# Turning q and k of the last chunk by DMA, holding one store behind a transpose, and a new order and layout: a fused transformer layer, forward and backward

## The chip, the cores and the metric

The kernel runs on one core of a Trainium2 chip (trn2). A core has a matrix engine (TensorE, PE in the profile; its weight loads are shown apart as PEld), a vector engine (VectorE, DVE), a scalar engine (ScalarE, ACT), a general engine (GpSimd, POOL) and a sync engine (SyncE, SP), which here only sends out DMA transfers. Each engine works through its own queue of instructions in order; semaphores tie the queues together. Sixteen DMA engines move data for all of them. SBUF is the on-chip memory with 128 partitions, PSUM holds the results of PE in 8 banks, HBM is the memory off the chip.

The metric is the device time of one execution in microseconds (us). Lower is better.

## What is computed

A pre-norm transformer layer over 2048 tokens of width 512, its output, and the gradients of seven of its inputs. Attention has 32 heads of width 16, and each token looks at 8 earlier tokens, two apart. The feed-forward part has 1792 hidden units.

```python
def _A_ref(x, wqkv, wo):                       # H = 32, Dh = 16, W = 8, dil = 2
    qkv = (x @ wqkv).reshape(B, S, 3, H, Dh).transpose(2, 0, 3, 1, 4)
    q, k, v = qkv[0], qkv[1], qkv[2]
    idx = pos[:, None] - (jnp.arange(W) * dil)[None, :]
    mask = idx >= 0
...
    logits = jnp.einsum("bhsd,bhswd->bhsw", q, kg) * scale
    attn = _softmax(jnp.where(mask[None, None, :, :], logits, -1e9), axis=-1)
    o = jnp.einsum("bhsw,bhswd->bhsd", attn, vg)
    return o.transpose(0, 2, 1, 3).reshape(B, S, D) @ wo

def _B_ref(x, w1, b1, w2, b2):
    h = _gelu(jnp.einsum("bsd,df->bsf", x, w1) + b1)
    return jnp.einsum("bsf,fd->bsd", h, w2) + b2

h = x + _A_ref(_layernorm(x), A_wqkv, A_wo)
h2 = h + _B_ref(_layernorm(h), B_w1, B_b1, B_w2, B_b2)
...
_out, _vjp = jax.vjp(_f, A_x, A_wqkv, A_wo, B_w1, B_b1, B_w2, B_b2)
_grads = _vjp(grad_out)                        # all in bf16
```

## The kernel before, in words

**Tiling.** The 2048 tokens are cut into four chunks of 512 (c = 0 to 3; "the fourth chunk" is c = 3, "the second" c = 1). A tile of a chunk is 128 partitions by 4 by 512 numbers of bf16, 512 KB. It is either token-major (a partition is a token) or feature-major (a partition is a feature); between the two lies a transpose, done either by PE in blocks of 128x128 against the identity, with an eviction from PSUM by ACT, or by a DMA that transposes (`dma_start_transpose`, wrapped by `xload`, line 290, always sent out by SP).

**Stages.** For each chunk, `p1_ln` normalises x, `p1_qkv` projects it to q, k and v, `p1_attn` makes the attention weights on VectorE (products) and PE (sums over a head's width), `p1_o` gathers v and makes the attention output, and `p1_h` multiplies by wo and normalises again. `p2_h`, `p2_dg`, `p2_out` and `p2_bwd` are the feed-forward part, forward and backward. `p3_go`, `p3_dots`, `p3_bands` and `p3_gl1` are the attention's backward pass. `wg_ffn` makes the weight gradients. All matrix products of the feed-forward part and of the weight gradients are groups of four or more matmuls on PE. A matmul with 128 columns of weights may be split into four with 32 (`mmul`, line 264), so the profile shows groups of 4 or of 16.

**Tensors in HBM.** The backward pass reads q, k, v and the gradient go as overlapping windows of tokens (`gather`, line 467, sent out by POOL). For that they are stored token-major in HBM: `q_d`, `k_d`, `v_d`, `go_d`. q and k come out of their projection feature-major. `p1_qkv` ends with a loop that turns k and then q: for a pair (name, chunk) in `TMD` (line 1191) by `tm_dma` (line 440), for all others by `to_tm_store` (line 425). Before, `TMD` names only the four chunks of go, so q and k of every chunk go through `to_tm_store`. That is two times per tensor and chunk: eight transposes on PE into one PSUM bank, one eviction of 128x1024 by ACT, one store of 256 KB by SP (`tm_store`).

`tm_dma` has two branches. With an offset of zero it turns the whole tile in one DMA; go takes that. The other branch sends four DMA transposes of 128 KB, one for each 128 features, into one tile, and then one store of 512 KB.

**The attention output.** `p1_o` builds the tile `ost` in four parts (`band`: a product on VectorE, a head sum on PE, a scaled copy by ACT). For the chunks in `FMO` = (1, 3) the finished tile is turned into `oT` by one DMA transpose (`turned`, line 547); PE turns it for the others. Last, `p1_o` stores `ost` to HBM from POOL's queue (line 727), for the weight gradient of wo at the end. `p1_h` multiplies `oT` by wo on PE.

**Order and memory.** Every step above is an operation in a list (`op`), numbered as the code creates it. It carries the engine, and the buffers that it reads (`r`) and writes (`w`), from which its predecessors follow; its costs and `soft` hints serve a planner that is not part of the kernel. The order in which the operations are issued is written out by hand in the tuple `ORDER` (line 1199), one number for each operation; each engine gets its own operations in that order. The place of every buffer in SBUF (in units of 64 bytes) or PSUM (the bank) is written out in `HOMES`. Two buffers that share a place make the later one wait for the last use of the earlier, and since SP works in order, everything behind it in SP's queue waits too.

Of the kernel before, what the change touches and what calls it, by code (L numbers as in the profile page):

```python
# [159 lines left out]
def kernel(  # L160
# [30 lines left out]
    NC = S // CH  # L191
# [39 lines left out]
    ln2_t, o_t = ([dram.tile([P, TPC, D], BF16, name=f"{n}_d{c}") for c in range(NC)] for n in ("ln2", "o"))  # L231
# [12 lines left out]
    sb, ps_, op, fx = pl.sb, pl.ps, pl.op, pl.fixed  # L244
# [40 lines left out]
    def store(dst, ap, src, src_ap, kb, key=None, skey=None, q="SP", tag="store", row=1):  # L285
        e, us = (SY, 0.45) if q == "SP" else (A, 0.45) if q == "ACT" else (G, 0.6)
        return op(q, us, lambda: e.dma_start(out=ap(), in_=src_ap()), r=[(src, skey)], w=[(dst, key)] if dst is not None else (),
                  dma=kb / (DMA_RATE if row <= 1 else WIDE_RATE), tag=tag, piece=0.006 + 0.0385 * row, mode=5)
# [151 lines left out]
    def tm_dma(fm, off, dst, c, back, tag, pm):  # L440

        st = sb("tm" + tag + "d", [P, 4, 512])
        r = c * CH + (RPAD if back else 0)
        if off:
# [268 lines left out]
    def p1_o(c):  # L713
        d = st_[c]
        oT = d["oT"] = sb("oT%d" % c, [P, DC, CH])
# [10 lines left out]
        if c < ORR:  # L726
            store(o_d[c], lambda: o_t[c][:], ost, lambda: ost(), 512, q="POOL", tag="ost", row=4)
# [463 lines left out]
TMD = (('go', 0), ('go', 1), ('go', 2), ('go', 3))  # L1191
# [144 lines left out]
```

## Time and profile before

| what | value |
|---|---|
| median of 3 runs | 551.72 us |
| lowest and highest run | 551.65 and 554.88 us |
| the profiled execution, its own time | 553.64 us |
| its span in the profile | 551.9 us |
| HBM read, written | 55.74 MB, 35.21 MB |
| bytes moved by DMA | 126.68 MB, mean 230 GB/s |

The span is what the profiler sees from the first to the last event; the execution's own time has 1.7 us more around it. "Busy" for PE is modelled, since its matmuls overlap one another, and "clock" is the share of TensorE's full speed that its throttle granted. A line such as `L268 PE MATMUL ps<-wo,oT 128*32 128x512 bf16 x48` reads: line 268 of the kernel, engine PE, what it writes and reads by the program's names, the size of the weights, the size of the moving operand, and how many. A number in brackets behind it is idle time of the engine ahead of it, with what ended it. `SPq` rows are transfers being sent out by SP; the time until the data has landed is given apart, as "to landing".

### The profile page before, as it was taken

Reading aid. Unit: us, or ns where it says so; the run is one execution under the profiler, and the core shown is the slowest. Engines: PE = TensorE matmul, PEld = TensorE weight load, DVE = VectorE, ACT = ScalarE, POOL = GpSimd, SP = SyncE. Lnnn points to the kernel's source line nnn. Section 1 sums busy time; section 2 is a strip of 40 time slices with the busy share of each in tenths; the row PEclk is TensorE's granted clock in tenths of the full one; section 3 lists DMA queues with packets and bytes.
Section 4 is the critical chain, followed back from the end, with each engine's and each line's share of the span. In section 5 each row is a group of like instructions: output and inputs, shape, how many; then the busy total and the mean of one; then the engine's idle time right before and its main releaser. Section 6 shows DMA issues by size and latency. Waiting matters only on the chain.

```text
span 551.9 us, 17462 instructions
## 1 busy us (share of the span) xinstructions
PE 538.8 (98%) x7764; PEld 286.7 (52%) x7764; DVE 494.2 (90%) x648; ACT 324.2 (59%) x507; POOL 25.8 (5%) x40
## 2 busy tenths in 40 slices
PE   7999999999989999999999999999999999999996
PEld 4756554444535445555555555465455555555542
DVE  7999999999979999999787089958899999999993
ACT  4987799989899876885341242034033376443521
POOL 1300100030001000000000000000010001000000
PEclk9999999999989999999999999999999999999999
DMA  8899998991597558679999999999999997888427
GB/s 279 226 291 281 417 302 190 201 332 83 74 235 251 137 98 197 201 121 214 197 191 219 182 194 192 291 218 281 213 279 425 335 338 284 355 290 187 128 60 190
DMA packets 195147, 126.68 MB, mean 230 GB/s; under 512 B 149760, under 2 KB 190656, under 8 KB 193024
## 3 DMA queue, kind: packets, MB, share of 16 engines
q1 hardware_dynamic: 189472, 81.79, 66.3%
q0 software_dynamic: 3408, 41.68, 19.8%
q10 hardware_dynamic: 2192, 2.10, 1.1%
q8 instruction: 60, 0.98, 0.8%
q14 instruction: 15, 0.12, 0.1%
HBM read 55.74 MB, written 35.21 MB: 165 GB/s over the span
## 4 chain that ended last, share of the span: by engine, by line
PE 55%; DVE 16%; ACT 4%; DMA 3%; issue 3%; SPq 2%; POOL 0%; ACTq 0%; DVEq 0%
PE ps L268 32%; PE ps L270 16%; PE ps L527 4%; DMA oT<-ost 2%; DVE xb L856 2%; DVE prbk L518 1%; DVE prbo L518 1%; DVE xb L803 1%; PE ps L487 1%; DVE prbv L518 1%; PE ps L543 1%; DVE x L799 1%; DVE st L360 1%; DVE h L747 1%; DVE h2s L828 1%
## 5 line engine op out<-in xcount | busy, mean ns | idle before, releaser
L479 DVE TENSOR_TENSOR prb<-got,vw 128x4096 bf16<-128x4096 bf16 x16 | 36.0, 2282 | 20.7 <-ACT got L297 13.8
L268 PE MATMUL ps<-w1T,xb 128*32 128x512 bf16 x896 | 53.1, 379 | 0.6 <-DVE h2s L828 0.4
L268 PE MATMUL ps<-goT,w2T 128*32 128x512 bf16 x832 | 50.5, 379 | 0.2 <-ACT xb L774 0.2
L297 ACT CAST wgs<-ps 128x512 bf16<-128x512 f32 (+1 forms) x30 | 16.2, 562 | 53.8 <-PE ps L270 30.4
L268 PE MATMUL ps<-w,gl 128*32 128x512 bf16 x776 | 46.3, 379 | 0.0
L856 DVE SCALAR_TENSOR_TENSOR xb<-xb,ps 128x512 bf16<-128x512 bf16 x56 | 36.9, 681 | 6.6 <-PE ps L268 6.4
L774 ACT ACTIVATE xb<-ps,b1c 128x512 bf16<-128x512 f32 x56 | 35.6, 703 | 10.1 <-PE ps L268 5.0
L268 PEld LDWEIGHTS <-xb 128*32 128x32 bf16 x896 | 26.2, 97 | 23.1 <-issue 1.2
L518 DVE TENSOR_TENSOR prbv<-Rv,cfv 128x4096 bf16<-128x4096 bf16 x16 | 35.7, 2284 | 1.4 <-PE ps L527 1.4
L518 DVE TENSOR_TENSOR prbq<-Rq,cfq 128x4096 bf16<-128x4096 bf16 x16 | 35.9, 2287 | 0.9 <-PE ps L270 0.4
L518 DVE TENSOR_TENSOR prbk<-Rk,cfk 128x4096 bf16<-128x4096 bf16 x16 | 35.9, 2284 | 0.3 <-PE ps L527 0.2
L518 DVE TENSOR_TENSOR prbo<-Ro,cfo 128x4096 bf16<-128x4096 bf16 x16 | 35.9, 2283 | 0.2
L479 DVE TENSOR_TENSOR prf<-qt,kt 128x4096 bf16<-128x4096 bf16 x16 | 35.7, 2283 | 0.0
L268 PEld LDWEIGHTS <-w2T 128*32 128x32 bf16 x832 | 24.0, 97 | 21.3 <-issue 0.5
L268 PEld LDWEIGHTS <-gl 128*32 128x32 bf16 x776 | 21.3, 97 | 21.1 <-ACT gl L777 1.3
L268 PE MATMUL ps<-wqkvT,gqkvT 128*32 128x512 bf16 x512 | 31.0, 379 | 0.0
L796 ACT ACTIVATE xb<-xb 128x2048 bf16<-128x2048 bf16 (+1 forms) x16 | 26.6, 1691 | 6.4 <-DVE xb L795 6.4
L626 PE MATMUL ps<-ln1T,wqk 128*32 128x512 bf16 x512 | 29.3, 381 | 0.7 <-ACT ln1T L297 0.7
L270 PE MATMUL ps<-ln2T,w 128*128 128x512 bf16 x120 | 27.4, 379 | 0.0
L792 ACT ACTIVATE x<-xb 128x2048 bf16<-128x2048 bf16 (+1 forms) x16 | 26.4, 1691 | 1.4 <-DVE h L747 1.3
L777 ACT ACTIVATE gl<-xb 128x2048 bf16<-128x2048 bf16 (+1 forms) x16 | 26.5, 1686 | 0.1
L561 ACT ACTIVATE gyr<-ps,rstd 128x512 bf16<-128x512 f32 x16 | 10.8, 677 | 23.5 <-PE ps L268 23.5
(199 smaller groups left out, 1085.7 us busy)
## 6 DMA issues: line engine op xcount, KB each, us to landing
Ro<-v_d POOLq DMA_DIRECT2D x4, 2304.0 KB, 11.6
Rq<-k_d POOLq DMA_DIRECT2D x4, 2304.0 KB, 11.5
Rv<-go_d POOLq DMA_DIRECT2D x4, 2304.0 KB, 13.9
Rk<-q_d POOLq DMA_DIRECT2D x4, 2304.0 KB, 14.1
g_d<-gl SPq DMA_DIRECT2D x9, 512.0 KB, 5.2
gh_d<-xb SPq DMA_DIRECT2D x9, 512.0 KB, 4.7
w<-in_B_w_dram SPq DMA_DIRECT2D x2, 1792.0 KB, 7.4
out_dram<-wgs SPq DMA_DIRECT2D x13, 256.0 KB, 4.7
```

The costliest lines, as they stand in the source:

```text
L268: T.matmul(out[32 * a:32 * a + 32, :], lhsT=l[:, 32 * a:32 * a + 32], rhs=r, start=start, stop=stop, skip_group_check=True)
L270: T.matmul(out, lhsT=l, rhs=r, start=start, stop=stop, skip_group_check=True)
L297: fn = lambda: A.copy(out=ap(), in_=pap())
L479: op("DVE", tt_us(4096), lambda g=g, pr=pr: V.tensor_tensor(out=pr(), in0=ql()[:, g, :].unsqueeze(1).to_broadcast([P, W, 512]), in1=_sub(k ...
L518: V.tensor_tensor(out=pr().rearrange("p a j (d h) -> p a j d h", h=H), in0=_sub(R()[:, o0, 0:1], [[st, 2], [512, 4], [32, DH], [1, H]]), i ...
L527: T.matmul(ps()[32 * j:32 * j + 32, :], lhsT=S4[:], rhs=pr()[:, hf, j, :], start=(hf == 0), stop=(hf == 1), skip_group_check=True)
L626: T.matmul(ps()[32 * a:32 * a + 32, gg * 512:(gg + 1) * 512], lhsT=_sub(wq_()[:, dc, 0:1], [[DH, H]], sel * D + 4 * g + a), rhs=rhs, start ...
L774: op("ACT", act_us(512, 1), lambda f=f, ps=ps, xb=xb, f0=f0: A.activation(out=xb()[:, f - f0, :], in_=ps(), func=ACT.Identity, bias=b1c[:, ...
L777: op("ACT", act_us(N), lambda xb=xb, gl=gl: A.activation(out=fl(gl), in_=fl(xb), func=ACT.Gelu_apprx_tanh), r=[xb], w=[gl], tag="gelu", mo ...
L792: op("ACT", act_us(N), lambda xb=xb, x2=x2: A.activation(out=fl(x2), in_=fl(xb), func=ACT.Square), r=[xb], w=[x2], tag="x2")
L796: op("ACT", act_us(N), lambda xb=xb: A.activation(out=fl(xb), in_=fl(xb), func=ACT.Tanh, scale=GC), w=[xb], tag="tanh", mode=6)
L856: op("DVE", 0.61, lambda f=f, ps=ps, z=z, f0=f0: V.scalar_tensor_tensor(out=z()[:, f - f0, :], in0=z()[:, f - f0, :], scalar=1.0, in1=ps() ...
```

## The change

Three things change in the code, and the two tuples are replaced.

- `TMD` gains ('q', 3) and ('k', 3). For these two, `tm_dma` takes its branch with four DMA transposes. The condition of that branch is now whether the tensor is q or k, since q has an offset of zero too. Twelve operations become ten: four groups of eight transposes on PE, four evictions on ACT and four stores of 256 KB on SP go; eight DMA transposes of 128 KB and two stores of 512 KB on SP come.
- `store` takes a list of further reads. The store of `ost` of the fourth chunk now also reads `oT`, so it waits on POOL until the DMA transpose of `ost` has landed.
- `ORDER` (1970 operations instead of 1972) and `HOMES` (883 buffers instead of 889) are new throughout. Operations made after the fourth chunk's q have numbers lower by two.

```diff
@@ -282,9 +282,9 @@
-    def store(dst, ap, src, src_ap, kb, key=None, skey=None, q="SP", tag="store", row=1):
+    def store(dst, ap, src, src_ap, kb, key=None, skey=None, q="SP", tag="store", row=1, more=()):
         e, us = (SY, 0.45) if q == "SP" else (A, 0.45) if q == "ACT" else (G, 0.6)
-        return op(q, us, lambda: e.dma_start(out=ap(), in_=src_ap()), r=[(src, skey)], w=[(dst, key)] if dst is not None else (),
+        return op(q, us, lambda: e.dma_start(out=ap(), in_=src_ap()), r=[(src, skey)] + list(more), w=[(dst, key)] if dst is not None else (),
                   dma=kb / (DMA_RATE if row <= 1 else WIDE_RATE), tag=tag, piece=0.006 + 0.0385 * row, mode=5)
@@ -441,7 +441,7 @@
         st = sb("tm" + tag + "d", [P, 4, 512])
         r = c * CH + (RPAD if back else 0)
-        if off:
+        if tag in "qk":
             for g in range(4):
                 xload(st, lambda g=g: st()[:, :, g * P:(g + 1) * P], lambda g=g: fm()[:, g, off:off + CH], 128, r=[(fm, g // 2)], key=g, tag="tmx" + tag)
             store(dst, lambda: dst()[r:r + CH, :].rearrange("(a p) d -> p a d", p=P), st, lambda: st(), 512, key=(c, 0), tag="tmst" + tag)
@@ -724,7 +724,7 @@
         d["ost"] = ost
         if c < ORR:
-            store(o_d[c], lambda: o_t[c][:], ost, lambda: ost(), 512, q="POOL", tag="ost", row=4)
+            store(o_d[c], lambda: o_t[c][:], ost, lambda: ost(), 512, q="POOL", tag="ost", row=4, more=[oT] if c == NC - 1 and c in FMO else ())
@@ -1188,7 +1188,7 @@
-TMD = (('go', 0), ('go', 1), ('go', 2), ('go', 3))
+TMD = (('go', 0), ('go', 1), ('go', 2), ('go', 3), ('q', 3), ('k', 3))
...
```

Read by their numbers, the operations that SP has round the transposes of `ost` stand as follows in the two orders (first sent first):

| round | before | after |
|---|---|---|
| second chunk's `oT` | w2 transpose, v store, x load, **oT**, three q stores, k store, q store | q transpose, w2 transpose, **oT**, x load, k store, two q transposes, q store |
| fourth chunk's `oT` | three stores of h2, w1 transpose, **oT**, w1 transpose, a small store, w1 transpose | x load, two stores of h2, x load, gelu store, x load, **oT**, w1 transpose, a small store, w1 transpose |

On PE, the operations between the last head sum of the fourth chunk's `ost` and its first matmul on `oT` are ten groups of four matmuls in the old order and thirteen in the new one. Between the same two points of the second chunk, the new order has one such group less. Ahead of the first matmul on the first chunk's `ghT` (the turned gradient in the backward pass), counted from the VectorE operation that completes its source, there were 24 groups' worth and there are now 8.

205 rows, old and new, of tables (HOMES, ORDER) are left out of this document.

## The prediction

> **What bounds the kernel now.** I read the page first, then the busy time by stretch, then the chain in order of time, and last the timelines of TensorE (PE), SP and GpSimd (POOL) round the one place where PE stands still.
>
> ```profile
> span 551.9 us, 17462 instructions
> PE 538.8 (98%) x7764; PEld 286.7 (52%) x7764; DVE 494.2 (90%) x648; ACT 324.2 (59%) x507; POOL 25.8 (5%) x40
> PE 55%; DVE 16%; ACT 4%; DMA 3%; issue 3%; SPq 2%; POOL 0%; ACTq 0%; DVEq 0%
> ```
>
> PE is busy for 98% of the span and carries most of the chain. So nearly every microsecond that leaves PE's work or its waits leaves the time, and nearly every new wait enters it. The stages differ, though. Busy us of each engine by stretch, then granted clock, DMA share and GB/s:
>
> ```profile
> core 0: us, PE busy (x) PEld busy (x) DVE busy (x) ACT busy (x) POOL busy (x), PEclk, DMA share, GB/s
> 80.00:100.00 20.00, 19.97 (x233) 9.55 (x231) 19.91 (x15) 19.76 (x27) 0.60 (x1) 1.00 0.87 180
> 100.00:120.00 20.00, 19.75 (x198) 9.81 (x199) 19.37 (x29) 19.62 (x25) 3.03 (x3) 1.00 0.99 268
> 154.00:156.00 2.00, 0.06 (x4) 0.06 (x8) 2.00 (x3) 1.99 (x2) 0.00 (x0) 1.00 1.35 145
> 156.00:158.00 2.00, 2.00 (x24) 0.85 (x28) 0.92 (x6) 2.00 (x2) 0.00 (x0) 0.58 0.80 174
> ```
>
> Between 80 and 120 us PE, DVE and ACT are all full. At 154 us PE does nothing for 2 us, and afterwards its clock is granted at 0.58. The chain says what it waited for:
>
> ```profile
> 126.40 1.24 DVE xb L803
> ...
> 129.70 3.61 PE ps L270 x16
> ...
> 145.99 9.90 DMA oT<-ost
> 155.94 44.55 PE ps L268 x788
> ```
>
> Up to 128 us the long pieces of the chain are DVE's, then PE's, then comes one transfer of 9.90 us, and after it PE again. That transfer is the DMA transpose of the fourth chunk's attention output (`turned`). Its surroundings on PE, SP and POOL:
>
> ```profile
> 144.70 0.62 PE L527 MATMUL ps<-prbo,S 128*32 128x512 bf16 x8
> 145.13 1.91 PE L268 MATMUL ps<-ln2T,w 128*32 128x512 bf16 x32
> ...
> 148.59 2.78 PE L268 MATMUL ps<-ln2T,w 128*32 128x512 bf16 x48
> 151.18 2.80 PE L268 MATMUL ps<-goT,w2T 128*32 128x512 bf16 x48
> 155.94 4.46 PE L268 MATMUL ps<-wo,oT 128*32 128x512 bf16 x48 [1.96 <-DMA oT<-ost]
> 160.22 1.04 PE L268 MATMUL ps<-goT,w2T 128*32 128x512 bf16 x16
> ```
>
> ```profile
> 143.87 1.51 SPq L291 DMA_TRANSPOSE w1T<-in_B_w_dram  x1
> 145.99 3.40 SPq L291 DMA_TRANSPOSE oT<-ost  x1
> 149.43 5.95 SPq L291 DMA_TRANSPOSE w1T<-in_B_w_dram  x1
> ```
>
> ```profile
> 146.26 0.59 POOL L287 DMA_DIRECT2D o_d<-ost  x1 [22.34 <-ACT ost L532]
> ```
>
> The transpose is sent out 2.1 us behind a transpose of w1 and 0.27 us ahead of the 512 KB store of the same tile.
>
> **The change, part by part.** *The wait at 154 us.* It costs twice. PE waits 1.96 us. Then 48 matmuls take 160.22 - 155.94 = 4.28 us, where 48 took 151.18 - 148.59 = 2.59 us: 1.69 us more at the lower clock. Together 3.65 us. The change acts on it in three ways. The store now waits for the transpose. In SP's new order (read by operation numbers) no w1 transpose is sent ahead of this one; a load of x and a store of gelu's output stand there, both free to leave long before, and the w1 transposes come behind. And PE's new order has 13 groups of four matmuls (each cut into 16 narrow ones) between the last head sum of the chunk and the first matmul on oT, not 10. A group takes 0.865 us (160 narrow ones from 145.13 to where 151.18 and its 48 would end, 153.77), so the cover grows from 8.65 to 11.2 us. The transpose leaves 0.86 us after PE is through with the head sum (145.13 to 145.99). Even with 9.90 us it lands after 10.8 us, inside 11.2. So I take the whole 3.65 us; the other end is 0, if it lands 2.6 us later than before.
>
> The skill gives another size. The Trainium skill, "TensorE: Matmul & The Clock Gate", section "HAM oscillation — how this bites in real kernels", warns of PE gaps above about 3.4 us. By that the clock would survive a gap of 1.96 us, the wait would be worth 2.0 us and the sum would end 1.7 us higher. The trace differs: clock 0.58 after the 1.96 us gap; the measurement decides.
>
> *The store's wait on POOL.* It leaves some 4 us later at the first chunk's landing time below. Behind it on POOL is only the power of the fourth chunk's second layernorm, which needs the very matmuls that read oT and so cannot run before the transpose has landed. The stored tile is read back in the last stage. I cost it at nothing; its cover is that distance, and without it the store's 0.59 us of issue would be the price.
>
> *Transposes off PE.* Sixteen 128x128 transposes each for q and k go, in four operations of 8.
>
> ```profile
> 88.45 0.61 PE L434 MATMUL ps<-ident,qt 128*128 128x128 bf16 x8
> 88.89 3.40 PE L270 MATMUL ps<-ln2T,w 128*128 128x512 bf16 x15
> ```
>
> ```profile
> L297 ACT COPY tmq<-ps 128x1024 bf16<-128x1024 bf16 x8 | 8.2, 1036 | 2.0 <-PE ps L434 2.0
> ```
>
> Each occupies PE for 88.89 - 88.45 = 0.44 us: 1.8 us in all. They lie in the first 130 us, where the chain is mostly DVE's. Counting the two orders, DVE has the same instructions ahead of the chunk's last product, plus two tiny ones. PE has the four operations less and one group more ahead of the last head sum. If that head sum comes at the same time, what is left of PE's work is one group shorter: 0.87 us. If PE sets that time, it is 1.8. I take 0.9, by the DVE rows of the chain; the ends are 0 and 1.8.
>
> *Evictions off ACT.* Four of 1.036 us (the row of q's; k's are the same copy): 4.1 us less, in a stage where ACT is 98% busy. Who waits there:
>
> ```profile
> DVE nm L376 <- POOL rstd L373: 0.3, 1, 0.3
> ACT xb L774 <- PE ps L270: 2.3, 4, 1.3
> ```
>
> From 80 to 145 us DVE waits for nobody worth naming, and ACT's longest wait is for PE. Full as it is, ACT is not what DVE waits for. I take 0; the other end is a gain of 4.1.
>
> *Eight DMA transposes on SP.* They move 1 MB from SBUF to SBUF; four stores of 256 KB become two of 512 KB. The trace has no transpose of 128 KB out of SBUF. The nearest are got's, of 512 KB:
>
> ```profile
> L291 SPq DMA_TRANSPOSE tmgod<-got x4: 1987/3050/9741, 320.4 to 380.9; - x4
> DMA to landing us min/median/max: 4.6/6.1/13.3
> ```
>
> ```profile
> L287 SPq DMA_DIRECT2D q_d<-tmq x8: 478/577/1548, 47.9 to 112.2; - x8
> ```
>
> One costs SP between 0.5 us (a quarter of the shortest) and 3.05 us (the median), eight of them 4 to 24 us, less two stores, 1.2 us. The results are wanted only by gathers of the last attention backward stage. What matters is who stands behind them in SP's queue: for k the load of w2, for q the transposes of w2 and of grad_out and, tightest, the second chunk's oT. Before, that was
>
> ```profile
> 107.57 1.90 SPq L291 DMA_TRANSPOSE oT<-ost  x1
> DMA to landing us min/median/max: 4.3/4.3/4.3
> 113.76 1.03 PE L270 MATMUL ps<-wo,oT 128*128 128x512 bf16 x4
> 114.62 0.62 PE L416 MATMUL ps<-ident,ln 128*128 128x128 bf16 x8
> ```
>
> It lands at 111.87, 1.9 us before PE comes to it. The new order has one group (114.62 - 113.76 = 0.86) less between, so the margin is 1.0 us. At 4.3 us it holds; I take 0. If it took 13.3 us like the slowest of got's, PE would wait 13.3 - (112.90 - 107.57) = 8.0 and lose 1.7 at the lower clock: the end is +9.7.
>
> *New order and homes.* Elsewhere the stages keep their sequence. Covers that shrank: eight groups (6.9 us) before the first matmul on ghT, where there were 24. Its landing times:
>
> ```profile
> DMA to landing us min/median/max: 4.5/5.3/6.2
> ```
>
> Still inside, by 0.7 us at worst; taken as 0, with 3.7 us at the other end, if it comes as late as oT did and the clock falls with it.
>
> *The sum.* The profiled execution took 553.64 us, 1.7 around its span: 553.64 - 1.96 - 1.69 - 0.9 = 549.1. The median of the runs, 551.72, lies 1.9 below that execution; whether it waits less or the profile adds time is not to be seen, so I take off half, 1.0: 548.1, rounded to 548.0, which is 0.7% under the median.
>
> **The rivals.** *ACT was what held the first stage.* For it: 19.76 and 19.62 us busy of 20. Against it: DVE's 19.91 and 19.37, and the waits. It would give the whole 4.1 us more: 543.9.
>
> *A tighter cover gives way a little.* The second chunk's oT lands in 9.9 us, as the fourth's did, with two q transposes and one of w2 ahead of it: wait 9.9 - 5.3 = 4.6 and 1.7 of clock, 548.0 + 6.3 = 554.3. Or ghT comes as late as the fourth chunk's oT did: 551.7.
>
> *The wait stays.* The w1 transpose behind oT, not the store or the one ahead, made it slow, and it gets slower by the cover that was added. Then only 0.9 goes: 551.7. Against it: the 9.90 us began with one w1 transpose ahead and the store beside, and both are gone.
>
> *Slower: SP's queue in the first stage.* The q transposes hold up SP and the DMA engines so that the second chunk's oT takes 13.3 us: 548.0 + 9.7 = 557.7. It decides from 557.2 on, a landing of 12.8 us. For it: the DMA share 0.99 there, the 9.74 us that one of got's held SP. Against: the q transposes are a quarter as large, and that one left 1.3 us behind a gather:
>
> ```profile
> 379.60 0.53 POOL L471 DMA_DIRECT2D Rv<-go_d  x1 [26.81 <-DVE prbq L518]
> 380.88 9.74 SPq L291 DMA_TRANSPOSE tmgod<-got  x1
> ```
>
> The Trainium skill speaks for it: "VectorE: DVE Perf Modes", section "The three transpose paths", has 390 ns for a 128x128 block on TensorE and 1309 ns by DMA, and its rules prefer TensorE where PSUM will do; no row here prices one such block.
>
> **How the numbers follow.** About 1% is what a measurement of this kernel can tell from no change. Forecast, 546.2 to 551: 0.45. ACT held the stage, below 546.2: 0.22. A cover gives way a little, 551 to 555: 0.15. The wait stays, about 551.7: 0.06. Slower, above 557.2: 0.12. Faster by over 1% (under 546.2) is the second with 0.04 from the forecast's lower edge, where the median runs had the full wait and PE the full 1.8: 0.26. Slower 0.12; within 1% the remaining 0.62. The range 543.9 to 554.3 leaves out the slower case and little else; the likeliest case's own is 546.2 to 551.
>
> **What would show it.** Right: no idle time of PE before the first matmul on the fourth chunk's oT, granted clock 1.00 from 140 to 180 us, the store on POOL some 4 to 10 us behind the transpose's issue; PE's count lower by 32; oT's last head sum within 1 us of 145. Wrong: PE idle before the second chunk's oT near 113 us, or before ghT near 310, with a clock under 1 behind it; SP busy without a break from 60 to 115 us; or a last head sum well before 144, which would say that ACT was the limit.

## The result: slower, and the profile after

| | median | runs |
|---|---|---|
| before | 552.56 us | 4 runs, 551.65 to 554.88 |
| after | 559.77 us | 4 runs, 557.50 to 563.47 |
| after over before | 1.0142 | 95% interval 1.0112 to 1.0173 |

The forecast was 548.0 us, 543.9 to 554.3. The profiled execution of the changed kernel took 559.96 us.

Ratios here are taken over runs within 1.5% of a kernel's fastest; the ranges below give every run, since the changed kernel and most of its variants scatter upwards by 10 us and more, while the 72 runs of the kernel before beside them, on the same chips, lie between 551.0 and 558.0 us.

The page of the changed kernel (span; busy time, share of the span and number of instructions):

```profile
span 558.2 us, 17856 instructions
PE 538.5 (96%) x7948; PEld 291.0 (52%) x7948; DVE 492.7 (88%) x648; ACT 320.4 (57%) x503; POOL 24.4 (4%) x40
```

PE has as much work as before (538.5 against 538.8 us). The 6.3 us of the span are idle time and clock. Windows of 40 us tell where. Before, then after (busy time of PE in the second column, then PEld, DVE, ACT, POOL; granted clock, DMA share, GB/s):

```profile
0.00:40.00 40.00, 35.57 (x409) 22.15 (x410) 35.97 (x64) 31.69 (x45) 6.96 (x12) 1.00 0.88 270
120.00:160.00 40.00, 37.92 (x426) 18.46 (x428) 37.06 (x54) 35.70 (x51) 2.00 (x2) 0.96 0.59 127
280.00:320.00 40.00, 39.76 (x740) 22.04 (x736) 20.95 (x54) 12.11 (x34) 0.00 (x0) 1.00 1.18 202
320.00:360.00 40.00, 40.00 (x465) 20.31 (x458) 36.79 (x36) 7.68 (x15) 0.60 (x1) 1.00 1.08 233
```

```profile
0.00:40.00 40.00, 37.68 (x448) 23.16 (x452) 36.64 (x67) 30.28 (x44) 4.98 (x12) 1.00 0.91 271
120.00:160.00 40.00, 37.34 (x433) 18.60 (x432) 36.73 (x54) 35.78 (x50) 2.00 (x2) 1.00 0.86 209
280.00:320.00 40.00, 38.43 (x715) 21.15 (x708) 23.94 (x54) 16.02 (x35) 0.00 (x0) 1.00 1.17 199
320.00:360.00 40.00, 33.40 (x498) 17.26 (x494) 28.12 (x27) 7.63 (x14) 0.60 (x1) 0.96 1.15 225
```

From 320 to 360 us PE idles 6.60 us where it idled for none, and the clock of 0.96 takes 40 x 0.04 = 1.6 us more: 8.2 us, more than the whole loss. They have two causes: 4.85 us of the idle time are one wait for VectorE's glf, and 1.75 us, ahead of it, one for gw2in. From 120 to 160 us the clock is back at 1.00 (1.6 us gained), but PE idles 2.66 us, 0.6 more than before, although the 1.96 us ahead of oT are gone. 280 to 320 us lose 1.3, the first 40 us gain 2.1. The other windows and the tail come to about nothing between them. PE's waits in the changed kernel name the culprits (total, times, longest):

```profile
PE ps L268 <- DVE glf L927: 4.9, 1, 4.9
PE ps L527 <- DVE prbo L518: 2.6, 2, 2.2
PE ps L270 <- DMA gw2in<-g_d: 1.7, 1, 1.7
...
PE ps L270 <- DMA oT<-ost: 0.4, 1, 0.4
```

**The forecast's own place.** The fourth chunk's oT: SP, POOL, PE.

```profile
147.13 2.91 SPq L291 DMA_TRANSPOSE oT<-ost  x1
```

```profile
147.40 0.59 POOL L287 DMA_DIRECT2D o_d<-ost  x1 [23.58 <-ACT ost L532]
```

```profile
158.01 1.91 PE L268 MATMUL ps<-wo,oT 128*32 128x512 bf16 x32
```

PE comes to oT 10.9 us after the transpose was issued and waits for nothing. The store, though, leaves 0.27 us behind the start of the transpose, as before, and was released by ACT: the added read sets the store's place in the written order and gives it no wait on the transpose.

**The new wait near 346 us.** SP, then DVE, of the changed kernel:

```profile
334.73 1.03 SPq L287 DMA_DIRECT2D go_d<-tmgod  x1
335.81 5.53 SPq L291 DMA_TRANSPOSE gw2in<-g_d  x1
341.44 8.48 SPq L291 DMA_TRANSPOSE gw1in<-gh_d  x1
350.02 1.70 SPq L287 DMA_DIRECT2D go_d<-tmgod  x2
```

```profile
341.54 4.48 DVE L479 TENSOR_TENSOR prb<-got,vw 128x4096 bf16<-128x4096 bf16 x2
353.74 1.22 DVE L927 TENSOR_TENSOR glf<-ps,attn 128x1024 bf16<-128x1024 f32 x1 [7.71 <-DMA go_d<-tmgod]
```

glf has nothing to do with tmgod. It lies on it: in the new HOMES the first two chunks' tmgod tiles (units 225 to 289 and 352 to 416) overlap glf (272 to 416). Before, they lay at 2614 and 32. So VectorE waits until the second tile's store is through, and that store stands behind two transposes that hold SP for 14 us. PE waits for glf:

```profile
355.02 3.33 PE L268 MATMUL ps<-gor,gw2in 128*32 128x512 bf16 x32 [4.85 <-DVE glf L927]
```

The 32 matmuls behind the wait take 3.33 us at the lower clock, where the 32 at 158.01 above take 1.91. An estimate from these lines: the wait for glf costs 4.85 + 1.42 = 6.3 us of the 8.2.

**The new wait near 130 us.**

```profile
111.61 3.96 SPq L291 DMA_TRANSPOSE tmqd<-qt  x2
...
116.69 0.59 SPq L282 DMA_DIRECT2D gor<-in_grad_out_dram  x1
128.73 0.37 SPq L287 DMA_DIRECT2D q_d<-tmqd  x1
129.15 1.18 SPq L287 DMA_DIRECT2D k_d<-tmk  x1
```

```profile
132.75 2.15 DVE L497 STREAM_TRANSPOSE cfo<-attn 128x512 bf16<-128x512 bf16 x2 [2.15 <-DMA k_d<-tmk]
```

The same pattern. cfo's new place overlaps the first chunk's old k tile (tmk). The store that frees it is behind q's store on SP, and that one waited 11.4 us for the turned q: SP sent nothing from 117.3 to 128.73.

### The profile page after: what moved, and what is told of

It is laid out like the page before. It is cut to its first block, busy times and chain, and to the rows that moved or that the text cites. A ratio compares the mean times of both kernels' runs of the same rounds, so it can differ in the third digit from the quotient of the medians.

```text
span 558.2 us, 17856 instructions
## 1 busy us (share of the span) xinstructions
PE 538.5 (96%) x7948; PEld 291.0 (52%) x7948; DVE 492.7 (88%) x648; ACT 320.4 (57%) x503; POOL 24.4 (4%) x40
## 4 chain that ended last, share of the span: by engine, by line
PE 50%; SPq 3%; DVE 2%; ACT 1%; DMA 1%; issue 0%; DVEq 0%
PE ps L268 31%; PE ps L270 13%; PE ps L527 4%; SPq L291 3%; PE ps L543 1%; PE ps L487 1%; ACT woT L1130 1%; DVE xb L856 1%; DMA go_d<-tmgod 1%; DVE u L566 0%; DVE glf L927 0%; DVE x L799 0%; SPq L287 0%; ACT gyr L561 0%; PE ps L919 0%
## 5 line engine op out<-in xcount | busy, mean ns | idle before, releaser
L479 DVE TENSOR_TENSOR prb<-got,vw 128x4096 bf16<-128x4096 bf16 x16 | 36.0, 2284 | 10.9 <-ACT got L297 10.3
L268 PE MATMUL ps<-gor,gw2in 128*32 128x512 bf16 x560 | 34.4, 391 | 4.9 <-DVE glf L927 4.9
L268 PEld LDWEIGHTS <-w2T 128*32 128x32 bf16 x832 | 24.7, 97 | 23.4 <-issue 4.2
L561 ACT ACTIVATE gyr<-ps,rstd 128x512 bf16<-128x512 f32 x16 | 10.9, 682 | 43.8 <-PE ps L268 39.1
L268 PEld LDWEIGHTS <-gl 128*32 128x32 bf16 x792 | 23.8, 97 | 19.4 <-issue 0.5
L268 PE MATMUL ps<-ln2T,w 128*32 128x512 bf16 x464 | 28.1, 379 | 0.0
L268 PEld LDWEIGHTS <-gw2in 128*32 128x32 bf16 x560 | 16.9, 99 | 19.6 <-issue 6.6
```

Of the source, the lines that this page charges most:

```text
L268: T.matmul(out[32 * a:32 * a + 32, :], lhsT=l[:, 32 * a:32 * a + 32], rhs=r, start=start, stop=stop, skip_group_check=True)
L479: op("DVE", tt_us(4096), lambda g=g, pr=pr: V.tensor_tensor(out=pr(), in0=ql()[:, g, :].unsqueeze(1).to_broadcast([P, W, 512]), in1=_sub(k ...
```

## The experiments

All runs, each beside the kernel before on the same chip (its medians there: 552.2 to 552.8 us):

| kernel | median, us | runs | lowest and highest, us |
|---|---|---|---|
| a_unchanged, a_unchanged2 (the changed kernel) | 570.7, 569.6 | 6, 6 | 557.9 to 584.5, 557.3 to 577.5 |
| a_store_ahead | 567.5 | 6 | 556.0 to 594.5 |
| a_q_store_behind | 573.7 | 6 | 560.8 to 577.6 |
| a_both | 569.1 | 11 | 553.0 to 588.8 |
| a_glf_free | 574.2 | 6 | 565.5 to 595.4 |
| a_q_early | 572.9 | 6 | 562.6 to 598.3 |
| a_fixed | 573.3 | 6 | 563.6 to 578.8 |
| a_plain | 559.4 | 6 | 557.5 to 563.9 |
| a_plain_glf | 553.2 | 13 | 550.4 to 576.3 |
| a_q_plain, a_k_plain | 564.3, 567.8 | 6, 6 | 556.1 to 571.7, 562.5 to 573.9 |
| a_pe_turns | 563.1 | 4 | 562.4 to 565.0 |
| a_pe_turns_glf | 555.8 | 5 | 554.5 to 556.2 |
| b_turns, b_turns2 | 561.5, 568.4 | 6, 6 | 555.9 to 574.5, 556.4 to 571.3 |
| b_plain | 557.7 | 6 | 555.4 to 567.1 |
| b_w1_behind | 553.1 | 12 | 552.3 to 556.4 |

The first variants scattered by up to 38 us, so the changed kernel was run again beside the next ones. It runs from 557.3 to 584.5 us; its first four runs were the lower end. A theory must explain the scatter too.

### Stores moved in SP's queue

```diff
 ORDER   # a_store_ahead: the second chunk's go_d store (1246) ahead of a gw1in transpose (1767)
-..., 1767, ..., 1246, ...
+..., 1246, 1767, ...
 ORDER   # a_q_store_behind: the q_d<-tmqd store (440) seven rows back, behind an h2 store (577)
-..., 440, ..., 577, ...
+..., 577, 440, ...
```

> The changed kernel with one DMA moved in SP's queue: the second chunk's go_d<-tmgod store goes ahead of the gw1in transpose that held SP for 8.48 us, nothing else. Theory 'laid over': VectorE's glf multiply waits 7.71 us only because glf lies on the place of that store's tile; the store is issued at about 341.5 instead of 350.0 us, lands before 347, VectorE's wait is under 1 us, PE's 4.85 us and the clock under 1 behind it go. PE was idle 6.6 us in 320 to 360 and lost about 1.6 more at clock 0.96, so the time falls by 4.9 to 8.2 us, to 551.5 to 555 where the changed kernel takes 559.8. Rival 'full queue': SP has too many transposes in that stretch; PE then waits as long for gw2in or gw1in, pushed back by the store, and the time stays at 557 or more.

> The changed kernel with the q_d<-tmqd store (512 KB, the fourth chunk's q) moved seven rows back in SP's queue, behind the k_d store, the h2 stores and the loads it stood in front of. Theory 'laid over': VectorE's 2.15 us before cfo and 0.57 us before a prbo go, PE's 2.2 us before bsum with them; the last head sum comes 1.5 to 2.7 us sooner and the time is 557 to 558.5 where the changed kernel takes 559.8. Rival 'the turn itself is late': the transposes of q land 12 to 16 us after issue, and the store, now seven rows back, releases tmqd's own place later: VectorE waits for q_d<-tmqd instead and the time is 559.5 or more.

> Both moves of the two runs above in one kernel. Theory 'laid over': the gains add, 559.8 - (4.9 to 8.2) - (1.3 to 2.7) = 549 to 553.6, middle 550.6: between no difference and 0.7% under the kernel before. The rivals: as one of them alone, or 557 and more.

By their medians all three fell on the rival's side. Under this scatter that is a weak test. In a_both a small gain isn't excluded: by its ratio it is at 1.0077 of the kernel before (1.0044 to 1.0109), the changed kernel at 1.0142 (1.0112 to 1.0173) in its first four runs and at 1.0128 (1.0056 to 1.0200) in a_unchanged2, on other chips. In a_store_ahead's profile, where VectorE waits 7.5 us before cfo and all behind it is about 9 us later:

```profile
350.73 0.62 SPq L287 DMA_DIRECT2D go_d<-tmgod  x1
351.45 11.14 SPq L291 DMA_TRANSPOSE gw1in<-gh_d  x1
```

```profile
362.73 1.23 DVE L927 TENSOR_TENSOR glf<-ps,attn 128x1024 bf16<-128x1024 f32 x1 [7.32 <-DMA go_d<-tmgod]
```

The store leaves ahead of the transpose now, and VectorE waits as long: it goes on 12.0 us after the issue, where it went on 3.7 us after it with the store behind (350.02 to 353.74 above). The DMA engines are full there (share 1.10 from 351 to 362 us), and the store is through when the transpose has been issued. So an earlier row of the queue needn't be an earlier landing. How much later is not general: stores of this kind issued behind the transposes took 9.2 us to land in a_pe_turns's profile, 9.6 in a_unchanged's and 10.0 in a_unchanged2's. In a_q_store_behind's profile, which is of its fastest run (560.8), the wait before cfo is gone and a wait of 1.5 us before prbo stands in its place; five of its six runs were above 572 us.

### glf's place freed

```diff
 HOMES   # a_glf_free, of the two tmgod tiles and of two prb tiles
-tmgod 225, tmgod 352, prb 1329, prb 1345
+tmgod 224, tmgod 1329, prb 288, prb 288
```

> The changed kernel with four homes changed and nothing else: the second chunk's tmgod tile goes from 352 to 1329, two prb tiles to 288 for it, the first chunk's tmgod tile from 225 to 224, so that glf (272 to 416) lies on the first chunk's tile alone, whose store is issued 15 us earlier. A side effect: the gather Rq (1185 to 1473) now waits for the second chunk's store, and starts near 350 instead of 340.79 us. Theory 'laid over': VectorE's wait before glf (7.71, 7.32, 6.93 us in the three profiles) falls under 1 us, PE loses under 2 us between 340 and 360 instead of 6.6, the clock stays at 1.00 there; 4.9 to 8.2 us less than the changed kernel in like runs, 551.5 to 555 against 559.8. Rival 'the transfers are the limit': PE waits as long for gw2in, or the gather comes late for prbq near 373; less than 2 us is gained.

> The changed kernel itself once more, beside the variants on the same chip, for its spread. Both theories: a median of 557 to 564 as in its first four runs (557.5 to 563.5). Theory 'the q turn is late': some runs lie far above, up to 590, since the landing of the q transposes (15.7 us in its first profile, 21.8 in a run of 567.6) sets when VectorE goes on near 130 us. Theory 'laid over alone': all runs within 4 us of each other, since the order and the places are the same in each.

The two from 320 to 400 us, a_unchanged first:

```profile
320.00:360.00 40.00, 38.10 (x669) 18.93 (x662) 24.61 (x22) 14.98 (x30) 0.60 (x1) 1.00 1.17 195
360.00:400.00 40.00, 34.80 (x368) 19.39 (x369) 30.91 (x30) 8.40 (x19) 0.32 (x1) 0.96 0.99 224
```

```profile
320.00:360.00 40.00, 39.84 (x677) 21.89 (x670) 26.68 (x23) 14.98 (x30) 0.00 (x0) 1.00 1.18 204
360.00:400.00 40.00, 39.12 (x502) 21.57 (x505) 35.37 (x33) 10.52 (x25) 1.13 (x2) 1.00 1.14 268
```

PE works 6.1 us more in these 80 us, and the clock keeps its 1.6. VectorE's wait for the store before glf, 5.92 us in a_unchanged, is gone: the place was its cause. Whether the total fell, six runs of each can't show, since those of either kernel lie 27 to 30 us apart; the cleaner pairs follow below. Another wait is far longer in these runs. VectorE, a_unchanged, and the landing times of q's turns (tmqd) and of the gathers of v (Ro) in the same profile:

```profile
145.68 2.15 DVE L497 STREAM_TRANSPOSE cfo<-attn 128x512 bf16<-128x512 bf16 x2 [12.24 <-DMA k_d<-tmk]
```

```profile
L291 SPq DMA_TRANSPOSE tmqd<-qt x4: 1202/1659/2655, 99.0 to 116.5; - x4
DMA to landing us min/median/max: 2.5/13.6/26.4
```

```profile
DMA to landing us min/median/max: 10.6/13.0/26.1
```

The 2.15 us at cfo are 12.24 here (9.9 in a_glf_free's profile). A q transpose and a gather of 2304 KB in flight beside it both take 26 us. In the first profile of the changed kernel the slowest of each took 15.7 and 15.4. Where the places and the order around q are the same, the time of the profiled run rises with the slowest of q's transposes: 15.7 us at 560.0, 18.8 at 563.1 (a_unchanged2), 21.8 at 567.6 (a_store_ahead), 22.8 at 571.0 (a_k_plain), 26.4 at 575.1 (a_unchanged). And a_unchanged2, on another chip, runs as long as a_unchanged, so it isn't one chip.

### q's turns sent earlier

```diff
 ORDER   # a_q_early; a_fixed is this with the homes of a_glf_free
-..., 439, ..., 437, ..., 436, ...
+..., 439, 437, 436, ...
```

> The changed kernel with two rows of SP's queue moved: the last two transposes of q go up beside the first two, ahead of the w2 transpose and the second chunk's oT, some 10 us before the 2304 KB gather is issued. Theory 'the q turn is late': all four have landed by 118, the q_d store is issued before 120 instead of 128.7, VectorE's wait before cfo (2.15 us, 7.5 us in a run of 567.6) goes and the long runs with it: the runs lie within 4 us of each other at 556 to 559. Its price: the second chunk's oT starts 2.4 us later, PE waits 0.4 to 2.8 us for it. Rival: the transfers are as slow wherever they are put; the landing stays at 13 us or more and the runs stay spread over 10 us and more.

> The places of a_glf_free and the order of a_q_early in one kernel. If both theories hold, the gains add: 559.8 - (4.9 to 8.2) - (1 to 2.7) = 549 to 554, with runs within 4 us of each other, at or under the kernel before (552.4). Rival 'the transfers are the limit': 555 and more.

q's turns land within 2.6 us there (3.7 in a_fixed), so their place counts. But nothing is won: 572.9 and 573.3. Ahead of oT they make PE wait 2.8 us for it, and other stores come late (VectorE's h waits 5.9 us for a k_d store, PE 4.8 us for w). The crowding moved to k's turns: the gather issued beside them at 73.9 us landed after 17.1 us in a_q_early's profile (570.8) and 23.4 in a_fixed's (578.8), where it took 9.5 in the first profile of the changed kernel. Why it meets them there is open.

### Copies in place of the turns

```diff
@@ tm_dma   # a_plain; a_q_plain and a_k_plain for one tensor only
-xload(st, lambda g=g: st()[:, :, g * P:(g + 1) * P], lambda g=g: fm()[:, g, off:off + CH], 128, ...)
+op("SP", 0.4, lambda g=g: SY.dma_start(out=st()[:, :, g * P:(g + 1) * P],
+     in_=fm()[:, g, off:off + CH].rearrange("p (a d) -> p a d", d=P)), ...)
```

> The changed kernel, with the eight transposes of q and k replaced by eight plain copies of the same 128 KB, in the same rows of SP's queue, with the same tiles, waits and stores. The copies don't turn the data, so the fourth chunk's q and k reach DRAM unturned: that part is left out. Theory 'turns load the transfers': a DMA transpose of 128 KB keeps the DMA engines busy far longer than a copy, in a stage where they are busy all the time already; without it the waits between 80 and 160 us go, and with them the spread: runs within 4 us of each other at 552 to 556, the wait before glf (6 to 8 us) still there. Rival 'rows and places': SP's extra rows, the places held longer and the new order make the waits, however the bytes are moved: median above 560, spread over 10 us as in the changed kernel (557.9 to 584.5 beside its variants).

> The same copies, and the four homes of a_glf_free. Theory 'turns load the transfers' together with 'laid over': the wait before glf goes too, 5 to 8 us less than a_plain: 546 to 550, under the kernel before (552.7). Rival 'rows and places': above 556. Rival 'the transfers are the limit' in the backward stage: within 2 us of a_plain.

The direction is the theory's, the size is not: 559.4 where 552 to 556 was expected. a_plain from 120 to 160 us, and its copies of q, then of k:

```profile
120.00:160.00 40.00, 39.13 (x470) 19.75 (x472) 38.70 (x59) 37.78 (x55) 2.00 (x2) 1.00 0.74 211
```

```profile
L446 SPq DMA_DIRECT2D tmqd<-qt x4: 644/664/680, 96.2 to 111.1; - x4
DMA to landing us min/median/max: 2.6/3.8/4.5
```

```profile
L446 SPq DMA_DIRECT2D tmkd<-kt x4: 612/659/696, 60.5 to 73.1; - x4
DMA to landing us min/median/max: 3.3/7.6/11.8
```

For k the landing is nearly that of the transposes in the first profile of the changed kernel:

```profile
DMA to landing us min/median/max: 4.0/8.4/12.9
```

So copies land sooner at q's place only; at both, SP issues one in 0.7 us where a transpose took 1.2 or more.

PE's idle time falls from 2.66 to 0.87 us (in a_unchanged PE was busy for 27.50 of the 40), and the scatter from 27 us to 6.4, over the 4 us expected. The median is 11 us below a_unchanged and 10 below a_unchanged2 (both on other chips), and level with the changed kernel's first four runs. With glf's place free as well, 6.3 us go: 553.2, ratio to the kernel before 1.0015 (0.9992 to 1.0037). Three of its 13 runs lay above 572, and the profile caught one (572.6 us). SP and PE there:

```profile
380.21 29.33 SPq L291 DMA_TRANSPOSE gw1in<-gh_d  x1
```

```profile
413.18 3.61 PE L268 MATMUL ps<-gw1in,ln 128*32 128x512 bf16 x32 [16.63 <-DMA gw1in<-gh_d]
```

One transpose, which the kernel before has too, held SP for 29.33 us, while a gather issued at 377.3 us was in flight; the slowest gather of that kind (Rv) landed after 32.2 us. So the scatter isn't q's alone. Every profile above 563 us shows a transpose that is stretched beside a stretched gather: q's beside the gather of v (a_unchanged, a_unchanged2, a_store_ahead, a_glf_free, a_k_plain), k's (a_q_early, a_fixed), here gw1in's, in b_turns2 below two of the backward stage. That the pairing makes the long runs is argued from these profiles, not shown: the kernel before sends its transpose of the turned gout (tmgod) beside the same gather Rv, where it held SP for 9.74 us and landed after 13.3, and its runs do not scatter so.

> The changed kernel with the four transposes of q replaced by plain copies (q of the fourth chunk reaches DRAM unturned); k's four transposes stay. Theory 'turns load the transfers', with q's beside the gather of 100 to 125 us as the worst of it: 559 to 562, spread under 6 us, as with all eight replaced (557.4 to 563.9). Rival 'k's turns do it': they fill the DMA queues from 60 to 75 us and the stores behind them come late: median above 563, spread over 10 us.

> The changed kernel with the four transposes of k replaced by plain copies (k of the fourth chunk reaches DRAM unturned); q's four transposes stay. Theory 'q's beside the gather': median above 563 and a spread over 10 us, nearly as in the changed kernel. Rival 'k's turns do it': 559 to 562, spread under 6 us.

> The changed kernel itself beside these three on one chip, as their base. Theory 'turns load the transfers': median 558 to 572 with runs over 10 us apart; the rival 'one chip was slow': within 3 us of 559.8, as in its first four runs.

All on one chip: copies for q leave 564.3, copies for k 567.8, all turned 569.6, each with runs 11 to 20 us apart. Neither theory wins. Of each pair of forecasts the one with the high median came true: q's turns alone bring the scatter back, and so do k's; the 3.5 us between the two medians are far inside the scatter. a_k_plain's profile (571.0) loses its time at q's place, with VectorE's wait of 9.0 us before cfo. Which stage made the high runs of a_q_plain was not seen; its profile is of a run of 556.1 with a clean first stage.

### The new order with TensorE's turns

```diff
 TMD   # a_pe_turns; a_pe_turns_glf has the homes of a_glf_free too
-(..., ('go', 3), ('q', 3), ('k', 3))
+(..., ('go', 3))
 HOMES
-tmkd 1921, tmqd 1070
+tmk 1921, tmk 1953, tmq 1070, tmq 1102 (PSUM banks 0, 6, 5, 6)
```

> The new order and homes, but the fourth chunk's q and k turned by TensorE as before (four groups of PE transposes, four evictions on ACT, four stores of 256 KB), in the places and near the rows of the transposes: the second part of the change without the first. Theories 'turns load the transfers' and 'laid over': no waits in the first stage, oT's wait of 3.65 us with its clock gone as predicted, the wait before glf there: 552.7 - 3.65 + (5 to 8) = 554 to 557, spread under 4 us. Rival 'rows and places': the first stage waits as in the changed kernel: above 560.

> The same with the four homes of a_glf_free: new order, turns by TensorE, glf's place free. Both theories: 554 to 557 less 5 to 8 = 547.5 to 551, that is 0.3% to 1% under the kernel before, spread under 4 us: the version that should beat both kernels. Rival 'the transfers are the limit' in the backward stage: within 2 us of a_pe_turns.

The code of the kernel before, with the new order and homes. No DMA transposes of q and k, no scatter: 2.5 and 1.7 us from lowest to highest. And freeing glf's place gives 563.1 - 555.8 = 7.3 us, the cleanest measure of it; PE is busy for 40.00 us from 320 to 360. But both lie above what was expected, a_pe_turns_glf at 1.0060 of the kernel before (1.0047 to 1.0073). It loses 2.5 us from 80 to 120 us, PE's waits for the evictions of the turned q and k (1.8 and 1.2 us), whose places in the order were my choice, and 2.4 from 280 to 320. The version that was to beat both does not.

### The kernel before, one part changed

```diff
 TMD   # b_turns; b_plain the same with copies
+('q', 3), ('k', 3)
 HOMES
-tmk 993, tmk 1025, tmq 416, tmq 448
+tmkd 993, tmqd 416
 ORDER   # b_w1_behind: one w1 transpose (511) behind the fourth chunk's oT (476) and the next w1 transpose
-..., 511, ..., 476, ..., 510, ...
+..., 476, ..., 510, 511, ...
```

> The kernel before with the turn of q and k alone: eight DMA transposes and two stores for the fourth chunk's four PE turns, four evictions and four stores, in the places of the old tiles, the eight transposes spread over SP's rows from 326 to 380 of the old order; the order and homes of all else as before. By the prediction's step the turn is worth 0.9 (0 to 1.8) us: 550.8 to 552.6 where the kernel before takes 552.6. Rival 'ACT held the first stage': 4.1 us off ACT come back as well, 547.5 to 549. Rival 'SP held up': w2T, the second chunk's oT or other rows come late behind the transposes, PE waits before them, 554 to 562.

> The kernel of b_turns (the kernel before with q and k of the fourth chunk turned by DMA, its own order and places), with the eight transposes replaced by plain copies of the same 128 KB in the same rows: q and k reach DRAM unturned. Theory 'turns load the transfers': without the turning the first stage stands as before: 551 to 554, spread under 4 us, at most 1% from the kernel before (552.4). Rival 'rows and places': eight more rows on SP, and kt's and qt's places held until a transfer has read them, cost the same however the bytes are moved: 558 to 563 like b_turns.

> b_turns once more beside it on the same chip, as its base. Theory 'turns load the transfers' and rival alike: a median of 558 to 565 and a spread over 10 us, as it had (555.9 to 574.5).

Turned by DMA, in the old order, the kernel takes 561.5 and 568.4 us. With copies on the chip of the latter it takes 557.7, 10.8 us less in the median, and 5.0 us remain without any turning. The ratios overlap (1.0138, 1.0080 to 1.0196, against 1.0086, 1.0063 to 1.0108): what the turning itself adds is mostly the high runs. How it adds them is open. b_turns2's profile (568.5) does not lose its time at the turns of q and k: up to 400 us PE idles 14.0 us, in b_plain 13.7. From 400 to 440 us PE is busy for 31.60 us at a clock of 0.91. SP and VectorE there:

```profile
385.39 20.77 SPq L291 DMA_TRANSPOSE tmgod<-got  x1
```

```profile
409.69 1.15 DVE L497 STREAM_TRANSPOSE cfq<-glf 128x512 bf16<-128x512 bf16 x1 [13.94 <-DMA tmgod<-got]
```

That is a transpose which the kernel before has too, beside the gather Rv issued at 383.33, which landed after 23.0 us. The 5.0 us that remain with copies are in VectorE, b_plain:

```profile
99.83 2.29 DVE L518 TENSOR_TENSOR prbo<-Ro,cfo 128x4096 bf16<-128x4096 bf16 x1 [4.00 <-DMA tmkd<-kt]
```

prbo waits until a transfer has read kt, whose place it takes. (In b_turns the same wait is 5.2 us.) So the rival "rows and places" holds for the 5 us. b_turns too came out in the range of its rival "SP held up" (554 to 562), though by this place and not by the second chunk's oT, for which PE waits 1.7 us.

> The kernel before with one row of SP's queue moved: the w1 transpose that stood ahead of the fourth chunk's oT goes behind it; no change of places, turns, store or cover. Theory 'the transpose ahead': that transpose (issued 2.1 us ahead, on the same DMA engines) made oT land after 9.9 us; without it oT lands in 5 to 8 us, inside the cover of 8.65, PE's wait of 1.96 us and the clock of 0.58 and 0.57 behind it go: 552.4 - 3.65 = 548.8, 548 to 550. Rival 'the cover': the three transposes of w1 behind it share the engines all the same, oT lands as late, and only the longer cover of the new order helped: 551.5 to 553.

The wait goes as the theory has it, and the time stays where the rival has it: ratio 1.0004 (0.9982 to 1.0026). PE, b_w1_behind:

```profile
154.28 2.77 PE L268 MATMUL ps<-wo,oT 128*32 128x512 bf16 x48 [0.29 <-DMA oT<-ost]
...
158.84 1.05 PE L268 MATMUL ps<-w,gl 128*32 128x512 bf16 x16 [0.93 <-ACT gl L777]
```

PE waits 0.29 us in place of 1.96 and its clock stays at 1.00. VectorE's first xb afterwards starts at 157.50 in place of 159.92, 2.4 us ahead. Then PE waits for ACT's gl, here and again 0.72 us at 185.94. VectorE waits for a store:

```profile
177.04 0.69 DVE L793 TENSOR_SCALAR ga<-x 128x2048 bf16<-128x2048 bf16 x1 [0.95 <-DMA g_d<-gl]
```

By VectorE's next ga (180.18 before, 178.98 here) the lead is 1.2 us.

## Why the prediction was wrong

- *The wait at 154 us.* Right that it goes, with the clock at 1.00 behind it. Wrong on the store, which waits for nothing and leaves 0.27 us behind the transpose's start, not 4 to 10. Over-sized: counted as 3.65 us, in b_w1_behind it left a lead of 2.4 us, then of 1.2 once PE waits for ACT's gelu and VectorE for a store, and nothing that the medians show.
- *The store's wait on POOL, 0.* The right number, since no such wait exists.
- *Transposes off PE, 0.9.* b_turns has the 32 fewer (x7732 against x7764) and the same busy time, 539.0 against 538.8, at a slightly lower granted clock (0.991 against 0.997 over the run); no gain is seen, and what the 32 are worth alone isn't shown. In the changed kernel the count rose to 7948, since the new order has the matmuls cut in other places (72 full ones became four each: -32 + 3 x 72 = 184).
- *Evictions off ACT, 0 with 4.1 as the other end.* From a_pe_turns_glf to a_plain_glf 2.6 us go, and PE's waits for those evictions, 3.0, are among them. So ACT's evictions cost something where PE waits for them. But no version, with or without them, is clear of the kernel before on the fast side (the lowest median is 553.1), so nothing bears out the rival of a full ACT (543.9); ACT's part was not tested alone.
- *Eight DMA transposes on SP, 0 with +9.7 as the other end.* The issue times were right (1.2 to 2.7 us each), and the second chunk's oT, which I had watched, cost PE 0.38 us. What I had priced was SP's time and one landing. The cost came by the stores behind them, through the places that these free, and by the transfers that share the DMA engines: 2.2 us of VectorE's wait in the first profile, 12.2 in another. The rival "SP's queue in the first stage", 557.7, at a chance of 0.12, came near the time by luck: what it priced, the second chunk's oT, did not happen, and most of the loss in the first profile lies in the backward stage.
- *New order and homes, 0.* This is the step that failed. I compared how many groups stand ahead of each transposed input, and never which new tile lies on which older one. glf on tmgod costs about 6.3 us by the first profile, 6.3 from a_plain to a_plain_glf and 7.3 from a_pe_turns to a_pe_turns_glf (both pairs also move two prb tiles). An estimate from these: without it the changed kernel's first four runs would have their median at 552.5 to 553.5, where the kernel before is. Put the other way, 552.56 and 6.3 to 7.3 make 558.9 to 559.9, and 559.77 was measured: of the 4.55 us counted as gained (3.65 and 0.9) nothing shows in the time.

The Trainium skill, "DMA: Bandwidth & Descriptors", section "Latency and other measured facts", gives DMA transposes 261 GB/s. By that, an estimate, 128 KB need 0.5 us. The runs differ: 2.4 us was the least, beside a gather up to 26.4. Its section "Queues, rings and completion order" has each DMA engine take turns between the queues packet by packet; that both the transpose and the gather stretch agrees with it (26.4 and 26.1 us), though no run here shows the turns themselves.

What stays open: what makes a transpose and a gather stretch to 16 us in one run and to 26 in another with the same order; why the kernel before, which has such a pair too, does not scatter so; how the turns of q and k bring high runs to b_turns2, whose profile lost its time elsewhere; and whether q and k could be turned by DMA at a place in this kernel where no gather is in flight, which was not tried.

## What to carry to other kernels

When places in SBUF are dealt out anew, list for every large tile what lay there last and which queue frees it; a place freed by a DMA is free only when that transfer has landed, and moving its row up a full queue needn't make it land sooner. Work moved from an engine to DMA has its price in what shares the DMA engines and in what its buffers hold up, and here it showed in the scatter of many runs more than in the first profile. A wait that is removed is worth what the next engine or transfer in line leaves of it: 1.2 of 3.65 us here.

## What the hardware showed that was not expected

- A transpose of 128 KB from SBUF to SBUF landed after 2.4 to 26.4 us at q's place, a copy of the same bytes in the same rows after 2.6 to 4.5; at k's place it was 4.0 to 12.9 in the first profile of the changed kernel and 3.3 to 11.8 for copies. SP needed 1.2 us at least to issue the one, 0.61 to 0.70 for the other.
- One DMA transpose held SP for 29.33 us with a gather beside it, another 20.77 (b_turns2); the first one's kind (gw1in) held SP for at most 7.96 us, and landed within 10.1, in the profile of the kernel before.
- VectorE went on 12.0 us after the issue of a store sent ahead of a transpose. It went on 3.7 us after the one sent behind it in the first profile; in three others such a store took 9.2 to 10.0 us to land.
